# Lag table of a long convolution: half of its rows kept as two unsummed parts, lag products for two channels at once

## The chip, the cores and the metric

The kernel runs on one core of a Trainium2 chip. The metric is the device time of one execution in microseconds, the median over runs. A core has a matrix engine (TensorE; PE in the profile, with its weight loads as PEld), a vector engine (VectorE, DVE), an activation engine (ScalarE, ACT), GpSimd (POOL, hardly used here) and a queue of DMA issues (SyncE, SP).

## The reference

The output is `g * a + (1 - g) * b`. Here `a` is segmented causal attention with a compressive memory (2048 tokens in 4 segments of 512, 32 heads of 16 channels), `b` a long convolution of the same input with a kernel K per channel, and `g` a gate per token. Only the part that makes K is touched:

```python
dt = jnp.exp(log_dt)[:, None]
A = A_re + 1j * A_im
Bc = B_re + 1j * B_im
Cc = C_re + 1j * C_im
logdA = dt * A
dB = dt * Bc
l = (lambda x, dt: x.astype(dt))(jnp.arange(L), A_re.dtype)
P = jnp.exp(logdA[:, :, None] * l[None, None, :])
K = jnp.einsum('dn,dnl,dn->dl', Cc, P, dB).real
...
Yf = Uf * Kf[None, :, :, :]
```

There are 512 channels d, 128 states n and 2048 lags l. The lags are bf16 numbers, so that only 640 different ones occur. The kernel computes K at these alone, and the convolution as a transform over blocks.

## The kernel before

**Order by hand.** The program is a list of operations (PE, ACT, DVE, DMA). A search made ahead of time chose the sequence in which all of them are issued, and for operations that ACT or DVE can do (evacuations of PSUM and copies) which of the two does them; it stands in the string `ORDER`, one number for each operation, with `a` or `v` for the engine and the buffer slots behind slashes. `Sched.replay` (L235) puts each operation in its engine's program in this sequence, and `Sched.emit` adds the semaphores. The cost expressions beside the operations (`("V2", 256 * n)`, `c_pe("C", ...)`) are for that search and change nothing in the program. Every matmul is recorded at L686, every DMA at L222, evacuations at L226 (ACT) and L227 (DVE), evacuations with a scale at L229 and L230.

**Attention.** For each of 4 segments and 4 groups of heads: projections of q and k; five score products (`scores`, L1007) with 16 or 32 rows in four row strips of the array, all into one PSUM buffer of four banks; an exp over all of it (L1068, ACT, 80 of them); a mask product (L1080, DVE); products with v (17 columns each); normalisation (L1040 to L1043).

**K's tables.** `ssm_prep` transposes the six parameter arrays so that states are on partitions and channels in columns, and evacuates them (three evacuations of 1024 columns); `ssm_powers` squares exp(logdA) step by step; `ssm_cb` multiplies C by dB. `tables(c)` runs for c = 0 to 3, a quarter of the channels (128) each. A lag is written as the sum of one of 20 exponents (`F_EXP`) and one of 32 (`G_EXP`). F holds the powers for the 20, G those for the 32, times C dB; each element is complex (two planes) and has 128 channels, thus 256 values on each partition. `cmul` makes n new elements out of n known ones, a complex product in three DVE instructions of 256 n elements: the source times the real part of the power into the table (L1165), the source times the imaginary part into `t2` (L1168), and the sum of both with the planes of `t2` exchanged (L1172). There are 13 such calls a table: three with n = 1, four with n = 2, three with n = 4 and three with n = 8.

**Lag products.** For every channel, two products over the 128 states (real and imaginary plane) give 32 x 20 lags: G's 32 columns of that channel are the weights, F's 20 columns move. Four channels, 32 apart, stand in four column groups of the array. That is 256 matmuls a table, issued in 8 groups of 32. Two evacuations of 320 columns bring them to `kex` (two buffers), four DMAs to `KTT`, from which the convolution's K products read. F and G have one buffer each, so the next table begins when the lag products of this one are done.

**Convolution and end.** 32 units of K product (5 x 512 columns), elementwise product Y (L1281), inverse product V (2 x 512 columns), with their evacuations; then the final products with `wo` and the transform's last step. All K products need all four tables.

Of the kernel before, what the change touches and what calls it, by code (L numbers as in the profile page):

```python
# [7 lines left out]
ACT = mybir.ActivationFunctionType  # L8
# [360 lines left out]
0/0 10/0 9/1 23/0/0 24v 15/0 29/0 31/0 38/1 32/2 30/3 33/4 13/2 14/3 27/4/1 39/5 37/6 34 35 40/7 54/0 57/1 6/0 36  # L369
193/0 4/0 41 42 43 44/8 48/0 45/9 46/10 12/4 47 49/11 53/0 50/12 17/0 61/1 59/0 62v/0 51/13 58a/0 60 71/1 52 65/2 11/5  # L370
55/2 56v 73/2 7/0 74v/1 25/3/2 26a 200/5/0/0 201a 250/0/1/1 72 83/3 1247/1 1250/6/0 214/1/0/0 28v 215 75 86v/2 205/0
85/3 173/4 3/0 21/0 66/5 16/0 253/2/0 84 95/0 178/6 20/0 18/0 97/7 98a/3 1226/0 176/1 1/0 251a 96 107/2 63 181/3
1248/7 254a 109/0 1249a 22/0 99 110v/4 202 67 189/0 108 377/0 208/3 190 177/0 252 203/0/1 204a 174/0 196/2 255/0/1/1
191 1251a 119/2 240/0/0 87 79/1 241 120/2 111 209a 122v/5 100 121 123 394/3/1 179/1 256 175 257 133/3 182 88 242
996v/0 395a 131/2 124 132 219/0/1 220 221 146a/6 77/0 998v/0 134v/7 192/0 1003/0 135 143/3 206/3 76 995v 212/0 1002
228/0/2 217 64 994v 1004 145/7 997v 213a 112 1008 1009/1 144 216 1252 229 230 78 1010 210/0 211a 1000/0 223/0/3 224
197/0 198/0 1015/1 147 158v/8 1014 999 136 1016 157/4 207a 235/1 1229/2/1 159 89/2 1001 1012/1 225 222/0 1017 155/3
1230a 1237/3/0 1018/0 1238a 799/0 266/0/1 267 293/2/2/2 226 156 1005 227 231 199/0 268 1011 91/0 1013 236/0/3 167a/9
148 1026 294a 237 588/0 589/3 590 160 168 1020 238 1021/1 232/0 169 90 233 334/2/0/0 335a 1019 1227/3 1228a 234/0
262/0/2 263 1231 264 337/2/2 338a 1022 800/3 239 243 244 1239/0 1240a 245/1 1241 101/0 1029 271/0/3 272 1024/0 273 801  # L380
378/2 246 379 1023 296/0/1 1234/3/1 247 1232/2 1233a 283/0/0 1025 284 297a 391 258 1235a 285 218/1/0 1033/1 102/6 103
113/3 295 1032 259 1258/2/0 1006/0 1259a 1034 1236 260/0 265/0 115/2 1030/1 1244/3/1 279/0/2 280 281 1245a 1242/1
1243a 269 1260/2 1007 1261a 270 1262 274 275/2 1031 1036/0 1027/1 307/0/1 308 309 278/3 282 286 287 1035 288/3
298/1/0/0 299 276 248/2 1037 249a/0 114 125/2 320/0/3 321 322 1028 1038/2/0 300 301 289 127/3 290/1 180 1039 1040 336
1246 126 1041 1042v 139/7 339/1/1/1 340 341 1263/3/0 194 1264a 303/0/2 304 1043/2 1044 277 137/0 1253/3/1 1265/1 138
342 1045 1046 305 151/4 291/0 1254a 1052v/0 1055v 324/0/0 68v/0 325 1056v/0 1053v 302/3 1054v 1060 343 1061/0 292a
1057 1047a 1051/0 326 104v/3 1062 383/0/1/1 384a 306/2 105 346/0/2 1066 1058/1 347 1067/0 1059 344 1268/0 80v/1 1070/1
1255/3 106 1068 1266a 1267 1063 81 310 311 348 1073/0 400/0/0/0 1069 401 116v/4 1072 443/1/0 1071 1256a 1257 444a
312/0/1 1074 313 314 386/3/1 402 1078 490/1/2/2 491a 92a/5 349/0 387a 1079/1 1076/0 350/0/2 351 352 1080 1075 1082/1
# [72 lines left out]
def fft_consts():  # L462
# [35 lines left out]
    return W1, M2, N2, G2  # L498


F_EXP = [1, 3, 5, 7, 2, 4, 6, 8, 258, 260, 262, 264, 516, 520, 772, 776, 1032, 1288, 1544, 1800]
G_EXP = [8 * j for j in range(32)]


# [20 lines left out]
def build_graph(nc, es, A_x, A_wq, A_wk, A_wv, A_wo, A_beta, B_A_re, B_A_im, B_B_re, B_B_im,  # L525
# [95 lines left out]
    zsP = mkpool("zs", 2048, 2)  # L621
    H1 = a
    Z1T = Tile(S.pool('Z1', H1, 2048, 1, 0), F32)
    a += 13 * 1024
    H2 = a
    V2aP = mkpool("V2a", 16384, 1)
    T0 = a
# [802 lines left out]
```

## Time and profile before

| | us |
|---|---|
| median of three runs (304.58 to 305.8) | 305.31 |
| the profiled execution | 305.48 |
| its span, first to last instruction | 303.3 |
| PE busy | 263.6 (87%) |
| DVE busy | 264.7 (87%) |
| ACT busy | 263.1 (87%) |
| mean granted PE clock | 0.958 |
| first K product of the convolution starts at | 172.64 |

The table products (L1165, L1168, L1172) take 33.9 + 33.7 + 33.8 us of DVE. The lag products are 1024 matmuls of 128 rows, 32 weight columns and 20 moving columns, with 10.4 us of busy time in which several of them overlap. A matmul record's duration is its whole way through the array; how fast products follow one another is read from their starts. Three engines are equally full over the whole span, which says nothing of the single stages: shares of the span are means over stages with different limits.

### The profile page before, as it was taken

What the parts mean: (1) busy time and instruction counts of PE and PEld (TensorE: products, weight loads), DVE (VectorE), ACT (ScalarE), POOL (GpSimd) and SP (SyncE); (2) the same over time, 40 slices, a digit from 0 to 9 for tenths busy, and PEclk for the clock granted to TensorE, in tenths of its full rate; (3) what the DMA queues carried; (4) which work ended last, traced back from release to release, by engine and by line L of the source; (5) the groups of instructions that cost most, each with busy time, mean ns of one, the idle gap of its engine ahead of it and who ended that gap; (6) DMA issues with size and microseconds to landing.
All of it is one profiled execution on the core that took longest, in us unless ns stands there. A gap on an engine that the chain in (4) does not pass through costs nothing.

```text
span 303.3 us, 9592 instructions
## 1 busy us (share of the span) xinstructions
PE 263.6 (87%) x4078; PEld 150.3 (50%) x4078; DVE 264.7 (87%) x639; ACT 263.1 (87%) x315; POOL 3.2 (1%) x9
## 2 busy tenths in 40 slices
PE   2697698799687888788889999999999999999992
PEld 1442355665344544565446555555545455546551
DVE  2999999999999998999998799999999869957171
ACT  3999999999999899999989998998899999985321
POOL 2000000000000000000000000000000000000000
PEclk9999899789996879999979999999999999999999
DMA  6983722216012331630500516766767756741033
GB/s 150 276 216 90 130 73 71 71 28 185 19 52 53 111 98 40 197 93 17 134 2 18 145 59 197 208 197 180 210 169 212 200 157 187 208 143 46 11 152 126
DMA packets 45002, 37.37 MB, mean 123 GB/s; under 512 B 21408, under 2 KB 40864, under 8 KB 44960
## 3 DMA queue, kind: packets, MB, share of 16 engines
q1 hardware_dynamic: 44960, 36.77, 43.0%
q8 instruction: 32, 0.52, 0.7%
q14 instruction: 10, 0.08, 0.1%
HBM read 18.54 MB, written 6.29 MB: 82 GB/s over the span
## 4 chain that ended last, share of the span: by engine, by line
PE 52%; DVE 22%; ACT 17%; DMA 4%; issue 2%; SPq 1%; ACTq 0%
PE psum L686 51%; ACT sb L1068 9%; DVE sb L1168 5%; DVE sb L1172 5%; ACT sb L226 4%; DVE sb L1165 4%; DMA sb<-in_A_wo_dram 2%; DMA sb<-in_B_log_dt_dram 1%; ACT sb L794 1%; SPq L222 1%; DMA sb<-sb 1%; ACT sb L948 1%; ACT sb L802 1%; DVE sb L227 1%; DVE sb L1122 1%
## 5 line engine op out<-in xcount | busy, mean ns | idle before, releaser
L686 PE MATMUL psum<-sb 128*32 128x20 bf16 (+11 forms) x3990 | 256.4, 232 | 26.0 <-ACT sb L1068 15.0
L686 PEld LDWEIGHTS psum<-sb 128*128 128x128 bf16 (+3 forms) x3990 | 143.6, 97 | 136.6 <-ACT sb L1068 30.0
L1068 ACT ACTIVATE sb<-psum 128x2048 bf16<-128x2048 f32 x80 | 151.4, 1893 | 7.4 <-PE psum L686 6.4
L226 ACT ACTIVATE sb<-psum 128x512 bf16<-128x512 f32 (+2 forms) x152 | 86.1, 615 | 6.8 <-PE psum L686 6.2
L227 DVE CAST sb<-psum 128x512 bf16<-128x512 f32 (+1 forms) x50 | 32.9, 674 | 6.1 <-PE psum L686 5.6
L1165 DVE TENSOR_TENSOR sb<-sb 128x512 bf16<-128x512 bf16 (+3 forms) x52 | 33.9, 660 | 0.1
L1172 DVE TENSOR_TENSOR sb<-sb 128x512 bf16<-128x512 bf16 (+3 forms) x52 | 33.8, 662 | 0.2
L1168 DVE TENSOR_TENSOR sb<-sb 128x512 bf16<-128x512 bf16 (+3 forms) x52 | 33.7, 658 | 0.1
L1080 DVE TENSOR_TENSOR sb<-sb 128x1024 bf16<-128x1024 bf16 (+1 forms) x40 | 22.5, 575 | 1.1 <-ACT sb L1068 0.8
L1281 DVE TENSOR_TENSOR sb<-sb 128x1024 bf16<-128x1024 bf16 x32 | 21.8, 685 | 1.2 <-ACT sb L226 0.8
L229 ACT ACTIVATE sb<-psum,sb 128x512 bf16<-128x512 f32 (+1 forms) x8 | 5.4, 688 | 13.4 <-PE psum L686 13.4
L1043 DVE TENSOR_TENSOR sb<-psum,sb 128x256 bf16<-128x256 f32 x32 | 13.2, 419 | 0.4
L230 DVE TENSOR_SCALAR sb<-psum,sb 128x512 f32<-128x512 f32 (+1 forms) x8 | 6.0, 748 | 8.4 <-PE psum L686 8.3
L794 ACT ACTIVATE sb<-sb 128x512 f32<-128x512 f32 x18 | 11.7, 667 | 0.0
L1040 DVE RECIPROCAL sb<-psum 128x16 f32<-128x16 f32 x32 | 8.0, 250 | 1.7 <-PE psum L686 1.7
L742 PE MATMUL psum<-sb 128*128 128x128 bf16 x24 | 3.1, 309 | 6.8 <-DMA sb<-in_B_A_re_dram 4.1
L1122 DVE TENSOR_TENSOR sb<-psum,sb 128x512 bf16<-128x512 f32 x12 | 8.3, 688 | 0.3
L1338 DVE SCALAR_TENSOR_TENSOR sb<-psum,sb 128x512 bf16<-128x512 f32 x8 | 5.5, 746 | 3.0 <-PE psum L686 3.0
L948 ACT ACTIVATE sb<-psum 128x512 bf16<-128x512 bf16 x12 | 7.7, 638 | 0.5 <-PE psum L945 0.4
L795 DVE TENSOR_TENSOR sb<-sb 128x256 f32<-128x256 f32 x18 | 7.4, 416 | 0.5 <-ACT sb L794 0.5
L999 ACT ACTIVATE sb<-sb 128x512 bf16<-128x512 bf16 x12 | 7.6, 633 | 0.0
L796 DVE SCALAR_TENSOR_TENSOR sb<-sb 128x256 f32<-128x256 f32 x18 | 7.5, 417 | 0.0
(67 smaller groups left out, 105.1 us busy)
## 6 DMA issues: line engine op xcount, KB each, us to landing
sb<-sb SPq DMA_DIRECT2D x64, 128.0 KB, 3.1
sb<-c_DN SPq DMA_DIRECT2D x32, 224.0 KB, 3.1
scr_Z<-sb SPq DMA_DIRECT2D x16, 256.0 KB, 2.4
sb<-scr_Z SPq DMA_DIRECT2D x16, 256.0 KB, 3.5
sb<-in_A_x_dram SPq DMA_DIRECT2D x5, 512.0 KB, 4.6
out_dram<-sb SPq DMA_DIRECT2D x8, 256.0 KB, 2.0
sb<-sb SPq DMA_DIRECT2D x20, 64.0 KB, 2.2
sb<-c_M SPq DMA_DIRECT2D x4, 256.0 KB, 4.4
```

The source lines that it names most:

```text
L226: fa = lambda e: e.activation(dst(), src(), ACT.Copy)
L227: fd = lambda e: e.tensor_copy(dst(), src())
L686: mm = lambda e, o_, l, r_, st, sp, **kw: e.matmul(o_, lhsT=l, rhs=r_, start=st, stop=sp, skip_group_check=True, **kw)
L794: op("ACT", ("As", 512), lambda e, sq=sq, Z=Z: e.activation(ap(sq, n=512), ap(Z, n=512), ACT.Square), r=[Z], w=[sq], key=PW[h] + PWS * k)
L1043: op("DVE", ("V1", 256), lambda e: e.tensor_tensor(ap(o1, gi * 16, [[128, 4], [32, 4], [1, 16]]), ap(T, dims=[[68, 4], [17, 4], [1, 16]]), ...
L1068: o = op("ACT", ("Ax", 2048), lambda e, P=P, pT=pT: e.activation(ap(pT, n=2048), ap(P, n=2048), ACT.Exp, scale=0.25), r=[P], w=[pT])
L1080: op("DVE", ("V2", 128 * nb), lambda e, pT=pT, dims=dims: e.tensor_tensor(ap(pT, dims=dims + [[1, 128]]), ap(pT, dims=dims + [[1, 128]]), ...
L1122: op("DVE", ("V1", 512), lambda e: e.tensor_tensor(ap(o2, 0, [[128, 4], [16, 8], [1, 16]]), ap(P2, 0, [[256, 4], [17, 8], [1, 16]]), ap(R2 ...
L1165: op("DVE", ("V2", 256 * n), lambda e: e.tensor_tensor(run(tile, ne, dst, 1), run(tile, ne, src, sstep), ap(pw, cl * 512, [[2, 128], [0, n ...
L1168: op("DVE", ("V2", 256 * n), lambda e: e.tensor_tensor(run(t2, n, 0, 1), run(tile, ne, src, sstep), ap(pw, cl * 512 + 256, [[2, 128], [0, ...
L1172: op("DVE", ("V2", 256 * n), lambda e: e.tensor_tensor(D_(), D_(), ap(t2, n * 128, [[-n * 128, 2], [2 * n, 64], [1, 2 * n]]), ALU.add), r= ...
L1281: op("DVE", ("V2", 1024), lambda e, Y=Y, XAB=XAB, K3=K3, xo=xo: e.tensor_tensor(ap(Y, dims=[[512, 2], [1, 512]]), ap(XAB, xo, [[512, 2], [ ...
```

## The change

- `F_EXP` has the same 20 exponents in another sequence, so that two calls of `cmul` with n = 1 become one with n = 2. A table has 12 calls.
- G's rows change halves: the smaller 16 exponents are now rows 16 to 31, the larger ones (128 and up) rows 0 to 15. For rows 0 to 15 (two calls with n = 8) the third instruction of `cmul` is left out: the first part stays in G, the second in a new buffer `GB` in place of `t2`, and the lag products add them up in PSUM.
- The lag products take two neighbouring channels at once. Weights are G's 64 columns of both (two planes) and then GB's 32 columns of both (two planes); 40 columns of F move. Each product gives all pairs of the two channels, of which those of a channel with itself are used. Two pairs of channels stand side by side, in column positions 0 and 64. There are 256 matmuls a table as before, in groups of 32, and three evacuations (480, 480 and 320 columns). The four DMAs read every second partition.
- The transposed parameters and `dt` are written in a sequence of channels in which channels 32 apart become neighbours; the diagonal's products follow (16 of one column for 4).
- `kex` has one buffer of double size; the pools of squares, Z, V2a and Xs lie elsewhere, with three squares instead of four and six Z instead of eight.
- `ORDER` is another one throughout, with 1730 operations instead of 1746.

The diff, without the lines of `ORDER`:

```diff
--- before.py
+++ after.py
@@ -366,92 +366,91 @@
 ORDER = """
...
 """
@@ -498,8 +497,8 @@
     return W1, M2, N2, G2
 
 
-F_EXP = [1, 3, 5, 7, 2, 4, 6, 8, 258, 260, 262, 264, 516, 520, 772, 776, 1032, 1288, 1544, 1800]
-G_EXP = [8 * j for j in range(32)]
+F_EXP = [1, 3, 6, 8, 2, 4, 262, 264, 258, 260, 5, 7, 520, 516, 776, 772, 1032, 1288, 1544, 1800]
+G_EXP = [128 + 8 * j for j in range(16)] + [8 * j for j in range(16)]
 
 
 def dft_const():
@@ -621,15 +620,15 @@
     zsP = mkpool("zs", 2048, 2)
     H1 = a
     Z1T = Tile(S.pool('Z1', H1, 2048, 1, 0), F32)
-    a += 13 * 1024
-    H2 = a
-    V2aP = mkpool("V2a", 16384, 1)
+    a += 2048
+    GBP = mkpool("GB", 8192, 1)
+    a = H1 + 29 * 1024
     T0 = a
     FP = mkpool("F", 10240, 1)
     GP = mkpool("G", 16384, 1)
     t2P = mkpool("t2", 4096, 2)
     pwP = mkpool("pw", 2048, NPW)
-    kexP = mkpool("kex", 1280, 2)
+    kexP = mkpool("kex", 2560, 1)
     TEND = a
     S.room = 207 * 1024 - a
     assert a <= 207 * 1024, a - 207 * 1024
@@ -638,9 +637,9 @@
     ftP = mkpool("ft", 1024, 14, 0)
     pbP = mkpool("pb", 2048, 3, 0)
     dtP = mkpool("dt", 1024, 1, 0)
-    a = H2 - 8192
-    sqPs = [mkpool("sq", 2048, 4, 0)] * 2
-    ZPs = [mkpool("Z", 2048, 8, 0)] * 2
+    a = H1 + 10 * 1024
+    sqPs = [mkpool("sq", 2048, 3, 0)] * 2
+    ZPs = [mkpool("Z", 2048, 6, 0)] * 2
     a = PT0
     prP = mkpool("pr", 1024, 6, 0)
     ldP = mkpool("ldt", 1024, 1, 0)
@@ -650,8 +649,9 @@
     MP = mkpool("M", 2048, 3, 2)
     assert a <= H1, a - H1
     a = H1
+    V2aP = mkpool("V2a", 16384, 1, 2)
     XsPs = [mkpool("Xsa", 4096, 3, 2)]
-    assert a <= H2, a - H2
+    assert a <= T0, a - T0
     a = T0
     V2bP = mkpool("V2b", 16384, 1, 2)
     CDP = mkpool("CD", 1792, 4, 2)
@@ -744,10 +744,10 @@
             T = Tile(pbP, BF16)
             S.tag = "prm%d" % wj
             op("PE", c_pe("F", *[128] * 8), f, r=[praw[2 * wj], praw[2 * wj + 1], ident], w=[P], acq=[T])
-            S.evac(lambda T=T: ap(T, n=1024), lambda P=P: ap(P, n=1024), 1024, r=[P], w=[T], psum16=True)
+            S.evac(lambda T=T: ap(T, 0, [[64, 16], [2, 32], [1, 2]]), lambda P=P: ap(P, 0, [[64, 16], [1, 32], [32, 2]]), 1024, r=[P], w=[T], psum16=True)
             pb.append(T)
         dt = Tile(dtP, BF16)
-        op("ACT", ("Asx", 512), lambda e: e.activation(ap(dt, n=512), ap(ldt, n=512), ACT.Exp), r=[ldt], w=[dt])
+        op("ACT", ("Asx", 512), lambda e: e.activation(ap(dt, 0, [[64, 8], [2, 32], [1, 2]]), ap(ldt, 0, [[64, 8], [1, 32], [32, 2]]), ACT.Exp), r=[ldt], w=[dt])
         res = []
         ers = []
         st = []
@@ -831,7 +831,8 @@
 
         def f(e):
             for c in range(4):
-                i = mm(e, ap(P, c, n=1), ap(CBT, 512 + c * 128, n=128), ap(onesT, n=1), True, True)
+                for q in range(4):
+                    i = mm(e, ap(P, c, n=1, p0=32 * q, np_=32), ap(CBT, 512 + c * 128 + 64 * (q // 2) + q % 2, [[2, 32]]), ap(onesT, n=1), True, True, tile_position=(0, 32 * q))
             return i
         op("PE", c_pe("F", 1, 1, 1, 1), f, r=[onesT] + CBp, w=[P])
         op("DVE", ("V1", 4), lambda e: e.tensor_tensor(ap(dcolT, n=4), ap(P, n=4), ap(dskT, n=4), ALU.add), r=[P, dskT], w=[dcolT])
@@ -1152,6 +1153,9 @@
                 res.append(dct[e_])
             return res
 
+        GB = Tile(GBP, BF16)
+        gbp = [GB.part() for _ in range(2)]
+
         def cmul(tile, dct, ne, dst, src, sstep, n, k):
             pw = pws[(k, h)]
             S.key = k0 + TT * 0.8 * nstep[0] / 50
@@ -1160,62 +1164,71 @@
             nstep[1] += 1
             rd = parts(dct, tile, src, n, sstep)
             wr = parts(dct, tile, dst, n)
-            t2 = Tile(t2P, BF16)
+            top = tile is G and dst < 16
+            t2 = GB if top else Tile(t2P, BF16)
+            tn, t0 = (16, dst) if top else (n, 0)
             run = lambda T, E, e0, st: ap(T, 2 * e0, [[2 * E, 128], [2 * st, n], [1, 2]])
-            op("DVE", ("V2", 256 * n), lambda e: e.tensor_tensor(run(tile, ne, dst, 1), run(tile, ne, src, sstep),
+            v2 = "V2n1" if n == 1 else "V2"
+            op("DVE", (v2, 256 * n), lambda e: e.tensor_tensor(run(tile, ne, dst, 1), run(tile, ne, src, sstep),
                                                                  ap(pw, cl * 512, [[2, 128], [0, n], [1, 2]]), ALU.mult),
                r=rd + [pw], w=wr + [tile])
-            op("DVE", ("V2", 256 * n), lambda e: e.tensor_tensor(run(t2, n, 0, 1), run(tile, ne, src, sstep),
+            op("DVE", (v2, 256 * n), lambda e: e.tensor_tensor(run(t2, tn, t0, 1), run(tile, ne, src, sstep),
                                                                  ap(pw, cl * 512 + 256, [[2, 128], [0, n], [1, 2]]), ALU.mult),
-               r=rd + [pw], w=[t2])
+               r=rd + [pw], w=[gbp[dst // 8]] if top else [t2])
+            if top:
+                return
             D_ = lambda: ap(tile, 2 * dst, [[ne * 128, 2], [2 * ne, 64], [1, 2 * n]])
-            op("DVE", ("V2", 256 * n), lambda e: e.tensor_tensor(
+            op("DVE", (v2, 256 * n), lambda e: e.tensor_tensor(
                 D_(), D_(), ap(t2, n * 128, [[-n * 128, 2], [2 * n, 64], [1, 2 * n]]), ALU.add), r=[t2], w=wr)
         fm = lambda *a_: cmul(F, fp, NF, *a_)
         gm = lambda *a_: cmul(G, gp, NG, *a_)
         k0 = S.key
         nstep = [0, 0]
         S.tag = "tabc%d" % c
-        for e_, k_ in ((0, 0), (4, 1), (5, 2), (7, 3)):
+        for e_, k_ in ((0, 0), (4, 1), (5, 2), (3, 3)):
             S.evac(lambda e_=e_: ap(F, 2 * e_, [[FPL, 2], [2 * NF, 64], [1, 2]]),
                    lambda k_=k_: ap(pws[(k_, h)], cl * 512, [[256, 2], [2, 64], [1, 2]]), 256,
                    r=[pws[(k_, h)]], w=parts(fp, F, e_, 1), pw=[F], sb=True)
-        S.evac(lambda: ap(G, dims=[[GPL, 2], [2 * NG, 64], [1, 2]]), lambda: ap(CBT, d0, [[512, 2], [2, 64], [1, 2]]), 256,
-               r=[CBp[h]], w=parts(gp, G, 0, 1), pw=[G], sb=True)
-        fm(1, 0, 1, 1, 1)
-        gm(1, 0, 1, 1, 3)
-        fm(2, 0, 1, 2, 2)
-        gm(2, 0, 1, 2, 4)
-        fm(6, 4, 1, 1, 2)
-        gm(4, 0, 1, 4, 5)
-        gm(8, 0, 1, 8, 6)
-        fm(8, 4, 1, 4, 8)
-        fm(12, 5, 2, 4, 9)
-        gm(16, 0, 1, 8, 7)
-        gm(24, 8, 1, 8, 7)
-        fm(16, 13, 2, 2, 9)
+        S.evac(lambda: ap(G, 32, dims=[[GPL, 2], [2 * NG, 64], [1, 2]]), lambda: ap(CBT, d0, [[512, 2], [2, 64], [1, 2]]), 256,
+               r=[CBp[h]], w=parts(gp, G, 16, 1), pw=[G], sb=True)
+        fm(1, 0, 5, 2, 1)
+        gm(17, 16, 1, 1, 3)
+        fm(10, 0, 1, 2, 2)
+        gm(18, 16, 1, 2, 4)
+        gm(20, 16, 1, 4, 5)
+        gm(24, 16, 1, 8, 6)
+        fm(6, 2, 1, 4, 8)
+        fm(12, 3, 2, 4, 9)
+        gm(0, 16, 1, 8, 7)
+        gm(8, 24, 1, 8, 7)
+        fm(16, 12, 2, 2, 9)
         fm(18, 16, 1, 2, 9)
         fr = [fp[i] for i in range(NF)]
-        gr = [gp[i] for i in range(NG)]
+        gr = [gp[i] for i in range(NG)] + gbp
         kex = Tile(kexP, BF16)
         S.key = k0 + TT * 0.8
         S.tag = "lag%d" % c
-        for hf in range(2):
+        for b0, nb in ((0, 12), (12, 12), (24, 8)):
             P = S.ps()
-            for sl0 in range(0, 16, 4):
-                def f(e, P=P, hf=hf, sl0=sl0):
+            for sl0 in range(0, nb, 4):
+                def f(e, P=P, b0=b0, sl0=sl0):
                     for sl in range(sl0, sl0 + 4):
-                        for cc in range(2):
-                            for dq in range(4):
-                                dl = 32 * dq + 16 * hf + sl
-                                i = mm(e, ap(P, sl * NF, n=NF, p0=32 * dq, np_=32), ap(G, (1 - cc) * GPL + (dl // 2) * 2 * NG + dl % 2, [[2, NG]]),
-                                       ap(F, cc * FPL + (dl // 2) * 2 * NF + dl % 2, [[2, NF]]), cc == 0, cc == 1, tile_position=(0, 32 * dq))
+                        for q in range(2):
+                            for cc in range(2):
+                                for hh in range(2):
+                                    pr = 32 * hh + b0 + sl
+                                    if q == 0:
+                                        w, m = ap(G, (1 - cc) * GPL + pr * 2 * NG, n=2 * NG), 64
+                                    else:
+                                        w, m = ap(GB, cc * 2048 + pr * 32, n=32), 32
+                                    i = mm(e, ap(P, sl * 40, n=40, p0=64 * hh, np_=m), w,
+                                           ap(F, cc * FPL + pr * 2 * NF, [[1, 2], [2, NF]]), q == 0 and cc == 0, q == 1 and cc == 1, tile_position=(0, 64 * hh))
                     return i
-                op("PE", c_pe("C", *[20] * 8), f, r=fr + gr + [F, G], pw=[P], acq=[kex])
-            S.evac(lambda hf=hf: ap(kex, 16 * hf, [[32, NF], [1, 16]]), lambda P=P: ap(P, dims=[[1, NF], [NF, 16]]), 320, r=[P], pw=[kex])
+                op("PE", c_pe("C", *[40] * 32), f, r=fr + gr, pw=[P], acq=[kex])
+            S.evac(lambda b0=b0, nb=nb: ap(kex, b0, [[32, 40], [1, nb]]), lambda P=P, nb=nb: ap(P, dims=[[1, 40], [40, nb]]), 40 * nb, r=[P], pw=[kex])
         for dq in range(4):
             S.dma(lambda dq=dq: ap(KTT, (4 * c + dq) * 160, n=160),
-                  lambda dq=dq: ap(kex, n=640, p0=32 * dq, np_=32), 40960, r=[kex], pw=[KTp[c // 2]])
+                  lambda dq=dq: ap(kex, 640 * (dq % 2), n=640, p0=64 * (dq // 2) + dq % 2, np_=32, pstep=2), 40960, r=[kex], pw=[KTp[c // 2]])
 
     def conv(k0, dk):
         D = dft_const().reshape(128, 16, 2, 5, 128).transpose(2, 1, 0, 3, 4).reshape(32, 128, 640)
```

## The prediction

> **What bounds the kernel now.** I read the windows view first, cut where the chain of waits changes character: 13.57 us is the first projection, 172.64 us the first K product of the convolution. Columns: stretch, its length, then busy time (and instructions) of PE, PEld, DVE, ACT and POOL, the granted clock, the DMA share and GB/s.
>
> ```profile
> 13.57:165.99 152.42, 127.61 (x2568) 75.58 (x2569) 148.16 (x379) 146.45 (x183) 1.31 (x2) 0.92 0.32 86
> 165.99:172.64 6.65, 6.26 (x88) 3.65 (x82) 5.29 (x14) 6.29 (x7) 0.00 (x0) 1.00 0.45 110
> 172.64:298.05 125.41, 124.75 (x1388) 67.14 (x1388) 103.12 (x228) 102.44 (x114) 0.00 (x0) 1.00 0.55 162
> ```
>
> There are two kernels in one. In the first 152 us VectorE (DVE) is busy 97% and ScalarE (ACT) 96%, and TensorE (PE) has 25 us free. After the first K product PE is busy 124.75 of 125.41 us, and nothing else matters. Second, the groups of the first stretch:
>
> ```profile
> L686 PE MATMUL psum<-sb 128*32 128x20 bf16 (+10 forms) x2528 | 125.6, 218 | 25.0 <-ACT sb L1068 15.0 <-DVE sb L1043 3.0 <-DVE sb L1172 1.9
> L1068 ACT ACTIVATE sb<-psum 128x2048 bf16<-128x2048 f32 x45 | 85.6, 1903 | 2.4 <-PE psum L686 1.8
> ```
>
> Of PE's 25.0 us, 15.0 end at an exponential (L1068): all scores share one PSUM buffer of four banks, so PE cannot write the next scores before the exp has read these, and ACT's exp needs PE at once after. Third, the chain of waits where the stretches meet (start, length, what):
>
> ```profile
> 161.77 5.77 PE psum L686 x223
> ...
> 167.62 0.59 SPq L222
> ...
> 168.90 0.60 SPq L222
> ...
> 169.54 3.01 DMA sb<-sb
> 172.55 0.09 issue
> 172.64 1.65 PE psum L686 x21
> ```
>
> The last lag products, their evacuation, four DMA issues, a landing, then K. So the time is (when the last table's lag products are done) + 6.65 us + (PE's work from the first K on). Last, the prices, from the groups by form:
>
> ```profile
> L1172 DVE TENSOR_TENSOR sb<-sb 128x2048 bf16<-128x2048 bf16 x12 | 14.5, 1212 | 0.0
> ...
> L1172 DVE TENSOR_TENSOR sb<-sb 128x512 bf16<-128x512 bf16 x16 | 6.7, 419 | 0.0
> ...
> L1168 DVE TENSOR_TENSOR sb<-sb 128x512 bf16<-128x512 bf16 x16 | 6.6, 412 | 0.0
> L1165 DVE TENSOR_TENSOR sb<-sb 128x512 bf16<-128x512 bf16 x16 | 6.5, 415 | 0.0
> ...
> L1172 DVE TENSOR_TENSOR sb<-sb 128x256 bf16<-128x256 bf16 x12 | 5.0, 412 | 0.1
> L1165 DVE TENSOR_TENSOR sb<-sb 128x256 bf16<-128x256 bf16 x12 | 4.9, 410 | 0.0
> L1168 DVE TENSOR_TENSOR sb<-sb 128x256 bf16<-128x256 bf16 x12 | 4.8, 396 | 0.0
> ...
> L226 ACT ACTIVATE sb<-psum 128x320 bf16<-128x320 f32 x6 | 2.7, 447 | 0.1
> ```
>
> A product over one exponent (256 elements) costs what one over two does (512).
>
> **The change, part by part.** (1) *Sums left out.* The adds of two G calls of eight exponents go, in four tables: 8 x 1.212 = 9.7 us of DVE. (2) *F's sequence.* Two one-exponent calls become one of two: 8 x (410+396+412) - 4 x (415+412+419) ns = 4.8 us. DVE is freed of 14.5 us. (3) *Evacuations.* Instead of two of 320 elements a table there are two of 480 and one of 320. Between 447 ns (320) and 617 ns (512) a 480 costs about 590: 590+590+447-2x447 = 0.73 us a table, 2.9 us in all, nearly all on ACT. (4) *The new order* hands DVE some of ACT's evacuations: ACT has 162 instead of 172, DVE 103 instead of 89. Pricing every operation that stands before the first K by its row: ACT 180.2 -> 176.6 us (one exp less), DVE 195.9 -> 190.3. These are sums of means, which overlap; ACT's busy time is 0.91 of its sum, DVE's 0.85. So both engines have 3.3 and 4.8 us less to do before the first K; I take 4.0 us earlier, if PE keeps up. (5) *From the first K on* PE's work at its pace in the records (216 ns for 512 columns, 56 for 128, 25 for 17) is 122.1 us before and 121.2 after: -0.9. (6) *Small things.* The three parameter evacuations (683 ns on DVE, about 1 us on ACT) now read with a step of 32: between nothing and twice as long, +0.7 each, partly under the waits for input loads: 0. The diagonal has 16 products of one column for 4: 0.3 us, off the path. One kex buffer for two: the next table's evacuation comes over 15 us after these four DMAs, whose landing takes 2 to 3 us: 0; if the last of them were still queued, one landing, 3 us. The DMAs keep count and size and their last place before the first K. V2a and Xs lie elsewhere; what lies under them is done before their first evacuation: 0.
>
> (7) *The lag products* are the open price. There are 256 a table as before, but of another kind. Before: 32 weight columns, 20 moving columns, four side by side in four column groups. In the records four start every 27 ns at full clock (122 of them in 956 ns from 164.67 us): 32 of them, one group of the order, take 0.22 us. After: two side by side, and for every pair of channels four products with 64 weight columns and then four with 32. A group of 32 is thus eight batches of four. Low end: each pair of products costs a round of 27 ns, 16 x 27 = 0.43 us. High end: PE changes from a 64-column to a 32-column division at every batch, and a change costs what changes cost in this trace. Where lag products with nothing to wait for are followed by a full 128-column matmul, the next start comes 104 to 115 ns after the last one instead of 7 (97.396 to 97.511 us, 165.809 to 165.920); score products in four row strips followed by transposes: 317 ns instead of 216. So a batch takes 27 + 110 ns and a group 1.10 us, five times today's. No row shows a change from 64 to 32; every change of division in the trace is charged, so I take the high end. The 32 groups then add 32 x 0.88 = 28 us to PE in a stretch where it has 25 free.
>
> The Trainium skill, TensorEngine Tiling (Array Packing), section Key Properties, says that changing the tiling mode, not only the tile, drains TensorE; the rows of 104 to 115 ns agree, and by the rule the sum is the one below, without it that of rival A. The skill's page TensorE: Matmul & The Clock Gate, section on LDWEIGHTS, lets a weight load grow with its columns (P/1.2 ns), which fits the 27 ns round; 64 columns would then need 53 ns, an estimate of 0.65 us a group even where no change is charged, and 1.3 where it is.
>
> What a group of 1.10 us delays: behind the bursts stand scores, thus an exp. In the new order the groups come in bursts of 3, 5, 5, 3, 3, 3, 2, 5, 3. While PE is in one, ACT has one exp in hand (1.9 us) and about half of its other work per exp ((146.45 - 85.6)/45 = 1.35 us): 2.6 us. Bursts of five (5.5 us) leave ACT without work for 2.9 us, of three (3.3 us) for 0.7: 3 x 2.9 + 5 x 0.7 = 12.2 us. DVE cannot run ahead either, since the next table needs the F and G buffers that the lag products still read.
>
> **Sum**, on the profiled execution's span: 303.3 - 4.0 - 0.9 + 12.2 = 310.6 us; 2.2 us lie around the span (305.48 us) and the median of the runs is 0.2 lower: **312.6 us**.
>
> **Rivals.** *A, the changes of division are free* (64 and 32 columns are one mode, or the sequencer hides it). A burst of five takes 2.2 us, less than ACT has in hand; only the gains are left: 305.3 - 4.0 - 0.9 = 300.4 (299.6 by DVE's gain, 301.1 by ACT's). For it: lag products today overlap in four column groups without loss, and DVE is the fullest engine of the stretch. Against it: no change in the trace is free. It decides the sign: below some 0.7 us a group the bursts of five cost no more than 3 us and the kernel is faster. 30%. *B, the price is real, but hidden*: PE's 25 free us and the evacuations in hand cover the bursts but for some 4 us; 305.3 - 4.9 + 4.9 = 305.3. Against it: 15 of the 25 us are waits for the exp which a late score brings back. 11%. *C, PE becomes the bound of the first stretch*: 127.6 + 28 = 155.8 us of work, and the 15 us of waits at the exps stay: +18.4 - 0.9 = 322.8; a fuller PE would lose less at half clock (0.92 granted now), so some 320. For it: 155.8 is already over 152.4. 15%. The forecast: 44%.
>
> **Range and chances.** 299.5 to 321 us: the low end is A with DVE's gain, the high end C; 8 in 10 or a little more. The forecast's own range, from in-hand work of 1.9 us instead of 2.6 (18.1 us lost) to 3.5 (6 us lost), is 306.4 to 318.5. About 0.5% (1.5 us) is what a measurement of this kernel can tell from no change. Faster: A, 0.30; same: B, 0.11; slower: the forecast and C, 0.59.
>
> **What would show it.** The lag rows: 1024 products of 40 columns whose busy time is about 30 to 38 us (mine) or 14 (A) where 10.4 was; starts in batches of four with 110 ns between batches. In the first stretch ACT's idle before L1068 grows from 2 to over 12 us, released by PE, and the first K comes near 181 us (A: 169). The table products' busy time falls by 14.5 us whatever happens. PE's stretch from the first K on stays at 124 to 125 us. I am wrong if lag products of both widths follow each other at the even pace of 27 ns a round, or if ACT stays full beside slow ones.

## The result, and the profile after

| | before | after |
|---|---|---|
| median, us (4 runs each) | 304.94 (304.21 to 305.8) | 345.49 (343.68 to 347.29) |
| ratio, 95% interval | | 1.1328 (1.1257 to 1.14) |
| span of the profiled execution, us | 303.3 | 345.5 |
| mean granted PE clock | 0.958 | 0.897 |
| first K product of the convolution, us | 172.64 | 214.36 |

The direction was as forecast; the size was not: 40 us where 7 were forecast, outside the range. The windows view, cut at the first projection and at the first K product (columns as before: stretch, length, busy time and instructions of PE, PEld, DVE, ACT and POOL, granted clock, DMA share, GB/s), says at once where:

```profile
13.57:172.64 159.07, 133.87 (x2650) 79.23 (x2651) 153.46 (x392) 152.74 (x189) 1.31 (x2) 0.92 0.32 87
```

That is the first stretch before the change. After it:

```profile
13.57:214.36 200.79, 172.72 (x2658) 111.24 (x2684) 152.88 (x388) 152.60 (x185) 1.31 (x2) 0.83 0.27 74
214.36:340.00 125.64, 123.01 (x1347) 65.86 (x1364) 103.96 (x227) 100.73 (x109) 0.00 (x0) 1.00 0.54 153
```

From the first K product on nothing has changed (125.6 us for 125.4). All of the loss, 41.7 us, is ahead of it, and there VectorE and ScalarE are as busy as they were (152.9 and 152.6 us; before 153.5 and 152.7). It is PE that has 38.9 us more (172.7 for 133.9). In slices of 20 us the loss has places of its own. The first row is from the kernel before, the others from the changed one:

```profile
60.00:80.00 20.00, 18.16 (x374) 10.92 (x362) 19.61 (x51) 19.97 (x26) 0.00 (x0) 0.93 0.30 87
```

```profile
60.00:80.00 20.00, 18.52 (x321) 13.45 (x323) 9.48 (x30) 11.01 (x14) 0.00 (x0) 0.58 0.08 23
80.00:100.00 20.00, 14.91 (x213) 8.40 (x214) 19.91 (x40) 20.00 (x25) 0.00 (x0) 1.00 0.24 76
100.00:120.00 20.00, 19.62 (x342) 13.53 (x341) 9.86 (x38) 9.67 (x12) 0.65 (x1) 0.68 0.21 57
140.00:160.00 20.00, 18.39 (x316) 14.11 (x320) 10.73 (x35) 10.74 (x15) 0.00 (x0) 0.74 0.19 56
```

Between the lag products (80 to 100 us) DVE and ACT are full as before. In the slices that hold them both stand still half of the time, PE is busy, and its granted clock is 0.58 to 0.74. The groups, by form (line, engine, operation, operands, count, busy us, mean ns, idle before and what ended it). The first row is the exps of the kernel before:

```profile
L1068 ACT ACTIVATE sb<-psum 128x2048 bf16<-128x2048 f32 x80 | 151.4, 1893 | 7.4 <-PE psum L686 6.4
```

```profile
L686 PE MATMUL psum<-sb 128*64 128x40 bf16 x512 | 34.5, 214 | 3.0 <-DVE sb L1181 2.1 <-DVE sb L804 0.9
L686 PE MATMUL psum<-sb 128*32 128x40 bf16 x512 | 30.3, 197 | 0.0
...
L1069 ACT ACTIVATE sb<-psum 128x2048 bf16<-128x2048 f32 x80 | 151.0, 1887 | 17.0 <-PE psum L686 16.1
...
L226 ACT ACTIVATE sb<-psum 128x480 bf16<-128x480 f32 x7 | 4.0, 570 | 22.4 <-PE psum L686 22.4
```

The lag rows are busy for 34.5 and 30.3 us, where 30 to 38 for both together was forecast. ACT's idle time before the exps (L1069) has grown from 7.4 to 17.0 us (ahead of the first K product from 2.4 to 14.2), and 22.4 us more stand before the evacuations of the lag products themselves. The timeline around the second burst, of five groups, shows what one does (start, length, engine, line, operation; in brackets the idle time before it and who ended it):

```profile
61.45 1.13 ACT L226 ACTIVATE sb<-psum 128x480 bf16<-128x480 f32 x2 [2.73 <-PE psum L686]
61.88 10.46 PE L686 MATMUL psum<-sb 16*128 16x384 bf16 x184 [0.47 <-issue]
...
63.50 1.88 ACT L1069 ACTIVATE sb<-psum 128x2048 bf16<-128x2048 f32 x1 [0.40 <-PE psum L686]
...
68.81 0.57 ACT L226 ACTIVATE sb<-psum 128x480 bf16<-128x480 f32 x1 [3.44 <-PE psum L686]
72.07 0.44 ACT L226 ACTIVATE sb<-psum 128x320 bf16<-128x320 f32 x1 [2.69 <-PE psum L686]
72.07 0.30 DVE L227 COPY sb<-sb 128x256 bf16<-128x256 bf16 x1 [7.12 <-PE psum L686]
```

PE works for 10.46 us without a pause: a few scores and transposes, and then 8.0 us of lag products, named in the row by the first of the 184 only. ACT has one exp in that time (to 65.38 us) and then waits 3.44 and 2.69 us, each time for a bank of lag products; DVE waits 7.12 us with a copy that begins the next table and needs the buffers that the lag products still read. At 72.07 us both start again.

The starts of the products in the trace, in the burst near 100 us while it still has the full clock, show the price of one pair of channels. From the first of four products with 64 columns to the first with 32 it is 171 ns, from there to the next 64 it is 151, then 172 and 153. Two batches take 322 ns, a group of 32 products (four pairs) 1.29 us; at half clock a pair takes 406 ns, a group 1.62 us. From first to last start all nine bursts take 45.7 us; before the change the lag products took 8.0 (pauses over 0.3 us left out).

On the other side of the account the table's DVE groups are these:

```profile
L1172 DVE TENSOR_TENSOR sb<-sb 128x512 bf16<-128x512 bf16 x20 | 9.0, 451 | 0.0
L1175 DVE TENSOR_TENSOR sb<-sb 128x512 bf16<-128x512 bf16 x20 | 9.0, 448 | 0.0
L1172 DVE TENSOR_TENSOR sb<-sb 128x1024 bf16<-128x1024 bf16 x12 | 8.8, 737 | 1.1 <-DMA sb<-sb 1.1
...
L1181 DVE TENSOR_TENSOR sb<-sb 128x2048 bf16<-128x2048 bf16 x4 | 4.9, 1217 | 0.0
```

Four sums of 2048 elements are left of twelve, as the change says. But the multiplications of 512 and 1024 elements have become dearer (415 and 686 ns before); see the run of F's sequence alone. The rows of three experiments below are those of disturbed executions at a lower granted clock: "two changes" (315.25 us, the other three 310.6 to 311.1), "four changes" (325.92 us; of the others one took 322.95, two 317.8 and 318.1) and "the sums put back" (318.25 us, the fastest 309.28).

### The profile page after: what moved, and what is told of

The parts are those of the page before. It is cut to its first block, busy times and chain, and to the rows that moved or that the text cites. A ratio compares the mean times of both kernels' runs of the same rounds, so it can differ in the third digit from the quotient of the medians.

```text
span 345.5 us, 9550 instructions
## 1 busy us (share of the span) xinstructions
PE 301.0 (87%) x4042; PEld 181.4 (53%) x4090; DVE 264.8 (77%) x633; ACT 260.6 (75%) x305; POOL 3.2 (1%) x9
## 4 chain that ended last, share of the span: by engine, by line
PE 58%; DVE 26%; ACT 8%; DMA 4%; issue 2%; SPq 0%; DVEq 0%
PE psum L686 57%; DVE sb L1175 6%; DVE sb L1172 6%; ACT sb L1069 6%; DVE sb L1181 4%; ACT sb L226 2%; DVE sb L227 2%; DMA sb<-c_DN 1%; DMA sb<-in_B_log_dt_dram 1%; DVE sb L795 1%; DMA sb<-sb 1%; PE psum L946 1%; DVE sb L796 1%; DVE sb L804 1%; DVE sb L950 0%
## 5 line engine op out<-in xcount | busy, mean ns | idle before, releaser
L686 PE MATMUL psum<-sb 128*128 128x17 bf16 (+10 forms) x3954 | 293.3, 240 | 30.1 <-ACT sb L1069 13.7
L686 PEld LDWEIGHTS psum<-sb 128*128 128x128 bf16 (+4 forms) x4002 | 174.4, 103 | 147.6 <-ACT sb L1069 29.0
L1069 ACT ACTIVATE sb<-psum 128x2048 bf16<-128x2048 f32 x80 | 151.0, 1887 | 17.0 <-PE psum L686 16.1
L226 ACT ACTIVATE sb<-psum 128x512 bf16<-128x512 f32 (+2 forms) x145 | 82.9, 611 | 39.5 <-PE psum L686 39.0
L227 DVE CAST sb<-psum 128x512 bf16<-128x512 f32 (+1 forms) x61 | 41.0, 684 | 28.8 <-PE psum L686 24.4
L1172 DVE TENSOR_TENSOR sb<-sb 128x512 bf16<-128x512 bf16 (+3 forms) x48 | 33.6, 710 | 1.2 <-DMA sb<-sb 1.1
L1175 DVE TENSOR_TENSOR sb<-sb 128x512 bf16<-128x512 bf16 (+3 forms) x48 | 33.1, 707 | 0.1
L1081 DVE TENSOR_TENSOR sb<-sb 128x1024 bf16<-128x1024 bf16 (+1 forms) x40 | 22.6, 574 | 0.8 <-ACT sb L1069 0.6
L1181 DVE TENSOR_TENSOR sb<-sb 128x512 bf16<-128x512 bf16 (+3 forms) x40 | 22.6, 575 | 0.1
L229 ACT ACTIVATE sb<-psum,sb 128x512 f32<-128x512 f32 (+1 forms) x8 | 5.4, 688 | 14.0 <-PE psum L686 14.0
L227 DVE COPY sb<-sb 128x256 bf16<-128x256 bf16 x18 | 5.1, 317 | 12.0 <-PE psum L686 12.0
```

The source lines that it names most:

```text
L226: fa = lambda e: e.activation(dst(), src(), ACT.Copy)
L227: fd = lambda e: e.tensor_copy(dst(), src())
L686: mm = lambda e, o_, l, r_, st, sp, **kw: e.matmul(o_, lhsT=l, rhs=r_, start=st, stop=sp, skip_group_check=True, **kw)
L1069: o = op("ACT", ("Ax", 2048), lambda e, P=P, pT=pT: e.activation(ap(pT, n=2048), ap(P, n=2048), ACT.Exp, scale=0.25), r=[P], w=[pT])
L1081: op("DVE", ("V2", 128 * nb), lambda e, pT=pT, dims=dims: e.tensor_tensor(ap(pT, dims=dims + [[1, 128]]), ap(pT, dims=dims + [[1, 128]]), ...
L1172: op("DVE", (v2, 256 * n), lambda e: e.tensor_tensor(run(tile, ne, dst, 1), run(tile, ne, src, sstep), ap(pw, cl * 512, [[2, 128], [0, n], ...
```

## The experiments

Theory at the start: the change of width inside the lag products (64 columns, 32 columns, eight times a group) sets their pace, and the time follows the number of changes. Rivals: wider products cost more as such; the new order and buffers are at fault. The edits are to the changed kernel unless another is named. Those expectations that were written before the first results go by this price alone.

**Two changes a group.** All 64-column products of a group first, then its 32-column ones:

```diff
-                    for sl in range(sl0, sl0 + 4):
-                        for q in range(2):
+                    for q in range(2):
+                        for sl in range(sl0, sl0 + 4):
```

> Theory: the excess is the change between 64 and 32 weight columns. In the changed kernel's records a batch of 64-wide products starts 171 ns, of 32-wide ones 151 ns before the next batch, where rounds inside a batch take 53 and 40 ns; so a group of 32 costs 1.29 us at full clock. With all 64-wide products of a group first and then all 32-wide ones there are two changes a group instead of eight: 7 x 53 + 118 + 7 x 40 + 111 = 0.88 us, 13 us less over the 32 groups, or 16 at the half clock of these stretches: 330 to 333 us. Rival 1 (the wider products themselves, the changes free): the same products stand here, 343 to 347 us. Rival 2 (the new order and the moved buffers): also unchanged, 343 to 347.

Measured: 311.0 us (310.58 to 315.25), ratio 1.0155 (1.0099 to 1.0212). With nothing changed but the sequence of products, 34 of the 40 us are gone, far more than the theory had expected: what goes is not the price of the changes alone. One part is the pace between changes, 31.8 and 25 ns a round instead of the 53 and 40 behind a change: a group takes 0.67 us at full clock where 0.88 was expected. The rest is PE's other work up to the first K product, 118.6 us for 127.0 in the profiled executions, with 30.4 us at half clock for 72.9.

**Four changes a group.** The same by two pairs of channels:

```diff
-                    for sl in range(sl0, sl0 + 4):
-                        for q in range(2):
+                    for q, sl in [(q, s + t) for s in (sl0, sl0 + 2) for q in range(2) for t in range(2)]:
+                        if True:
```

> Two pairs' 64-wide products, then their 32-wide ones: four changes a group, between the kernels with two (311.0 us) and eight (345.5). Theory (each change costs some 75 to 110 ns of a drained array, and the first stretch has nothing to cover it): a group lasts about 0.85 us where those two have 0.63 and 1.29 at full clock, 7 us more of products than with two changes: 317 to 323 us. Rival (the clock: the drained array is granted half its clock, and only the eight changes drain it enough): like two changes, 310 to 314 us, at 28 to 35 us of half clock instead of the changed kernel's 73; or, if the clock falls here too, 328 or more.

Measured: 320.55 us (317.8 to 325.92), ratio 1.0454 (1.0395 to 1.0513). As expected, by then from the two runs with two and no changes.

**One change a bank.** All 64-column products of a PSUM bank, then all its 32-column ones:

```diff
-                    for sl in range(sl0, sl0 + 4):
-                        for q in range(2):
+                    for q, sl in [(q, s) for q in range(2) for s in range(nb)][2 * sl0:2 * sl0 + 8]:
+                        if True:
```

> All 64-wide products of a PSUM bank (12 or 8 pairs), then all its 32-wide ones: about one change a group or less, the same sums as in the changed kernel. Theory: close to the kernel without any change (307.4 us): 306.5 to 309.5 us, some 0.53 us a group. Rival (alternation inside a group costs nothing by itself, and the kernel with two changes differs from the one with none by its narrower products): no better than 311.

Measured: 307.53 us (306.1 to 308.32), ratio 1.0106 (1.007 to 1.0141). It computes the same as the changed kernel and is 38 us faster, though not faster than the kernel before.

**No change inside a group.** The second part's products take 64 weight columns too, which adds wrong rows to the table:

```diff
-                                        w, m = ap(GB, cc * 2048 + pr * 32, n=32), 32
+                                        w, m = ap(GB, cc * 2048 + min(pr, 62) * 32, n=64), 64
```

> The second part's products take 64 weight columns too, so that the lower half of each table's rows gets a neighbouring pair's values added and the convolution is another one. No change of division is left inside a group. Theory: 16 rounds of 53 ns = 0.85 us a group, near the kernel with two changes: 329 to 332 us; starts evenly 53 ns apart in twos, no 110 ns gap. Rival 1 (wide products): more columns are loaded than in the changed kernel, so slower than it, 348 us or more. Rival 2 (order, buffers): 343 to 347.

Measured: 307.44 us (305.17 to 311.38), ratio 1.0054 (1.0018 to 1.009). More columns and no change: wider products as such are ruled out, and as with two changes the gain is far above the expected one. In the records two 64-column products side by side start every 31.8 ns.

**The second part left out.** Only the first part's products, 128 a table; the terms of `GB` are missing from the table:

```diff
-                        for q in range(2):
+                        for q in range(1):
...
-                                           ap(F, cc * FPL + pr * 2 * NF, [[1, 2], [2, NF]]), q == 0 and cc == 0, q == 1 and cc == 1, tile_position=(0, 64 * hh))
+                                           ap(F, cc * FPL + pr * 2 * NF, [[1, 2], [2, NF]]), q == 0 and cc == 0, cc == 1, tile_position=(0, 64 * hh))
```

> The second part's products are left out, so the upper half of the table's rows is not the sum. Products: 128 a table, eight rounds of 32 ns a group, 0.26 us, near the kernel before (0.26 us measured, with its waits). Theory (the lag products alone stand between the changed kernel and the gain worked out for DVE and the order): 300 to 303 us. Rival (the order or the slower table products and parameter evacuations cost the gain): 304.5 us or more, with the first K product no earlier than 171.5 us.

Measured: 301.3 us (299.81 to 302.61), ratio 0.9901 (0.9872 to 0.9929). Where the lag products take little more than before (9.7 us for 8.0), the kernel with its new order, buffers and DMAs is 3.7 us faster.

The dose, in one table (lag: from first to last start, summed over the bursts, pauses over 0.3 us left out; PE busy and free from 13.57 us to the first K product; the last five columns are of the profiled execution, which took 315.25 us with two changes and 325.92 with four):

| kernel | changes a group | time, us | lag, us | first K, us | PE busy | PE free | clock |
|---|---|---|---|---|---|---|---|
| before | | 304.94 | 8.0 | 172.64 | 133.9 | 25.2 | 0.92 |
| second part left out | 0 | 301.3 | 9.7 | 170.31 | 131.4 | 25.4 | 0.92 |
| no change | 0 | 307.44 | 17.5 | 173.56 | 133.2 | 26.8 | 0.97 |
| one change a bank | under 1 | 307.53 | 16.1 | 174.68 | 135.1 | 26.1 | 0.97 |
| two changes | 2 | 311.0 | 22.9 | 183.34 | 141.4 | 28.4 | 0.92 |
| four changes | 4 | 320.55 | 29.5 | 192.65 | 154.3 | 24.8 | 0.90 |
| after | 8 | 345.49 | 45.7 | 214.36 | 172.7 | 28.1 | 0.83 |

The rows of the windows view behind five of these lines, in this order: second part left out, no change, one change a bank, two changes, four changes.

```profile
13.57:170.31 156.74, 131.35 (x2170) 80.80 (x2169) 151.02 (x388) 149.76 (x183) 1.31 (x2) 0.92 0.35 92
```

```profile
13.57:173.56 159.99, 133.22 (x2657) 86.64 (x2684) 151.50 (x388) 150.35 (x184) 1.31 (x2) 0.97 0.33 89
```

```profile
13.57:174.68 161.11, 135.05 (x2682) 84.68 (x2681) 151.49 (x388) 150.75 (x183) 1.31 (x2) 0.97 0.33 88
```

```profile
13.57:183.34 169.77, 141.42 (x2655) 91.42 (x2682) 151.88 (x388) 151.05 (x184) 1.32 (x2) 0.92 0.31 83
```

```profile
13.57:192.65 179.08, 154.27 (x2684) 95.52 (x2683) 151.49 (x388) 151.07 (x182) 1.32 (x2) 0.90 0.30 82
```

The column to read is "PE free". Lag products of 9.7 to 45.7 us leave it at 25 to 28 us: no increase of PE's work has gone into PE's idle time. And from "no change" to "after", with one order and one division of labour, 28.2 us more of lag products move the first K by 40.8 us. PE's free time is 1.3 of it; the remaining 11.3 us are PE's other work, which goes from 133.2 - 17.5 = 115.7 to 172.7 - 45.7 = 127.0 us, while time at half clock goes from 14.9 to 72.9 us in the records. The first step of the dose looks different: from "second part left out" to "no change" 7.8 us more of lag products move the first K by only 3.3 us. That is not idle time put to use either, since PE's free time is 1.4 us longer; PE's other work is 6.0 us shorter there, with 14.9 us at half clock for 29.0. No run shows why the clock falls less.

**Only 32 columns.** A 64-column product as two of 32 side by side, 384 products a table, all of one width:

```diff
...
+                                    for lo in range(2 - q):
+                                        w = ap(GB, cc * 2048 + pr * 32, n=32) if q else ap(G, (1 - cc) * GPL + pr * 2 * NG + 32 * lo, n=32)
...
```

> The 64 columns of the first part are taken as two products of 32 in two column groups; 384 products a table, all 32 wide, the same sums. Theory: four rounds a pair of channels at 27 to 40 ns, 0.43 to 0.64 us a group instead of 1.29, 14 to 20 us in all instead of the 45.7 us that the nine bursts last: the first K product comes 25 to 32 us earlier, 313 to 321 us; if what is left of the bursts is hidden again behind the exps, down to 302. Rival 1 (wide products: 40 moving columns and more of them): no better than 335. Rival 2 (order, buffers): 343 to 347.

Measured: 316.62 us (315.86 to 317.67), ratio 1.0346 (1.0292 to 1.04). Within the expected range; but the products run at some 8.4 ns each and take 13.1 us (pauses over 0.3 us left out), less than the 16.1 in "one change a bank", and still the first K comes at 182.89 us. The next run shows why.

**One channel at a time**, as before the change, with G's 32 columns and then `GB`'s 16, 512 products a table:

```diff
-                                        w, m = ap(G, (1 - cc) * GPL + pr * 2 * NG, n=2 * NG), 64
+                                        w, m = ap(G, (1 - cc) * GPL + pr * 2 * NG + b, [[2, NG]]), 32
...
-                                        w, m = ap(GB, cc * 2048 + pr * 32, n=32), 32
+                                        w, m = ap(GB, cc * 2048 + pr * 32 + b, [[2, 16]]), 16
...
```

> The two parts stay unsummed, but each channel is taken alone again: 32 and then 16 weight columns, 20 moving ones, four column groups, 512 products a table, evacuations of 240, 240 and 160 columns. No change of division. Theory: 128 rounds of 27 ns, 3.5 us a table, 14 us in all, and less evacuation: 0 to 5 us faster than the kernel with 32-wide pairs; 300 to 315 us. Rival 1 (wide products) predicts the same gain here, since none is left: this run does not tell it from the theory. Rival 2 (order, buffers): 343 to 347.

Measured: 329.85 us (329.33 to 330.81), ratio 1.0779 (1.0726 to 1.0833), outside what was expected. PE's waits (engine and what, released by; us in total, times, longest) show a thing that no other kernel has so much of:

```profile
PE psum L686 <- issue: 23.3, 22, 2.4
PE psum L686 <- ACT sb L1069: 13.4, 20, 2.0
```

For 23.3 us PE waits for nothing that the profile shows. The rows of the products, by form, say where:

```profile
L686 PE MATMUL psum<-sb 128*32 128x20 bf16 x1024 | 18.9, 180 | 17.3 <-issue 15.1 <-DVE sb L1181 1.2 <-DVE sb L804 0.9
L686 PE MATMUL psum<-sb 128*16 128x20 bf16 x1024 | 18.3, 174 | 3.3 <-issue 3.3
```

So 18.4 of the 23.3 us lie among the lag products; the first three stalls last 2.0, 2.2 and 2.2 us. Counting weight loads and matmuls, there are 255 and 256 PE instructions from one of them to the next (further on 251 to 256, 509 to 511, 1,019, 1,269 and 1,527 between stalls over 0.3 us among lag products: about 1, 2, 4, 5 and 6 times 256). "Only 32 columns" has 11.5 us of the same kind, the changed kernel 2.7. So this is not what the change lost its time to. It is of the size by which these two ways around the changes of width fall behind "one change a bank" (22.3 us for 23.3 of stalls, 9.1 for 11.5).

**F's sequence alone**, in the kernel before, with its order but for the 12 instructions that go:

```diff
-        fm(1, 0, 1, 1, 1)
+        fm(1, 0, 5, 2, 1)
...
-        fm(6, 4, 1, 1, 2)
...
-        fm(12, 5, 2, 4, 9)
+        fm(12, 3, 2, 4, 9)
```

> The kernel before with F's new sequence alone: two one-exponent calls become one of two, 12 calls a table, everything else and its order as before. Theory (DVE, the fullest engine of the first stretch, sets its end): 4.8 us less of DVE, 1 to 4 us of it in the time: 301 to 304 us. Rival (ACT is as full, 96%, and its work is the same): 304.5 to 306 us.

Measured: 304.74 us (303.22 to 306.46), ratio 0.9995 (0.9962 to 1.0028): nothing. The groups of this run show one reason:

```profile
L1188 DVE TENSOR_TENSOR sb<-sb 128x512 bf16<-128x512 bf16 x20 | 9.0, 453 | 0.0
L1191 DVE TENSOR_TENSOR sb<-sb 128x1024 bf16<-128x1024 bf16 x12 | 8.9, 744 | 0.0
...
L1188 DVE TENSOR_TENSOR sb<-sb 128x1024 bf16<-128x1024 bf16 x12 | 8.9, 742 | 0.0
```

Two calls are dearer in the new sequence. The call that reads F's columns 0 and 5, `fm(1, 0, 5, 2, 1)`, takes 586 to 616 ns a multiplication in all four tables, where other calls of 512 elements take some 415; the one that reads columns 3, 5, 7 and 9 takes 840 to 858 instead of the 685 of columns 5, 7, 9 and 11 before. By line, the three instructions of `cmul` are 33.8 + 33.6 + 32.5 = 99.9 us, for 101.4 before: 1.5 us freed instead of 4.8. In the changed kernel the same two groups stand at 451 and 737 ns. The rival, that ACT is as full as DVE and holds the time, is not settled by this run.

**The sums put back.** The changed kernel's order with the eight sums put in, and the whole table from the first part's products alone:

```diff
             if top:
+                D_ = lambda: ap(tile, 2 * dst, [[ne * 128, 2], [2 * ne, 64], [1, 2 * n]])
+                op("DVE", (v2, 256 * n), lambda e: e.tensor_tensor(
+                    D_(), D_(), ap(GB, 2048 + 2 * dst, [[-2048, 2], [32, 64], [1, 2 * n]]), ALU.add), r=[gbp[dst // 8]], w=wr)
                 return
...
-                        for q in range(2):
+                        for q in range(1):
...
```

> The changed kernel with its sums put back: VectorE adds the second part to rows 0 to 15 of G as before the change (8 instructions of 2048 elements more, just behind the two products), and the lag products take G's 64 columns of a channel pair only (128 products a table, no change of width). It computes the whole table; the sequence of F, the new order and the 14 evacuations given to VectorE stay. Theory: the gain that the run with the second part's products left out showed (301.3 us) is VectorE's time, and the new order has spent it on those evacuations; with 8 x 1.22 = 9.8 us of sums back the first K moves from 170.1 to 176 to 180 us and the time is 306.5 to 311 us. Rival: the gain is the new order's, and the sums were hidden: 300 to 303 us.

Measured: 309.28 to 318.25 us in six runs, five of them 317 to 318; too uneven for an interval. The lowest is 8.0 us above the median with the sums left out (301.3), so the rival (the order alone brings the gain) falls. The size rests on this one run, which is in the theory's range; the median of all six, 317.26 us, is above it. The first stretch of the profiled run (318.25 us):

```profile
13.57:186.38 172.81, 138.60 (x2169) 85.32 (x2168) 161.18 (x396) 150.61 (x183) 1.32 (x2) 0.87 0.31 82
```

DVE has 161.2 us of work here instead of 151.0, and PE is free for 34.2 us.

## Why the prediction was wrong

**The lag products' price** was right in its mechanism and too low: 1.29 us a group at full clock for 1.10. The gap from the last product of a batch to the next batch is 116 ns behind 64 columns and 110 behind 32, just as charged from neighbouring rows. What was too small is the round, two products side by side, in front of it: 27 ns were taken, from 32-column products with 20 moving columns, and the second round of a batch starts 52 and 39 ns after the first. (Even for the old products the prediction's own line, 122 starts in 956 ns, gives 31 ns for four and not 27.) Without changes a round takes 31.8 ns with 64 columns and 25 with 32, in the long runs of "one change a bank", so four products of each take 64 + 50 = 114 ns; with two changes they take 322, and a change costs 104 ns. Besides, half of the products ran at half clock. Instead of 28 us PE got 37.6 more.

**The cover is the step that failed**: "While PE is in one, ACT has one exp in hand (1.9 us) and about half of its other work per exp ...: 2.6 us", and with it "3 x 2.9 + 5 x 0.7 = 12.2 us". It hid 15.8 of the 28 us. The runs show no such cover: against 25.2 us before the change, PE's free time is between 24.8 and 28.4 us in every line of the table, and more where PE stalls. In the timeline above ACT did have its one exp, but the burst of five lasted 8.0 us instead of 5.5, and ACT waited 6.1 us in it instead of 2.9; DVE, to whose waits the forecast gave no number, stood for 7.1. The sum up to the first K was 28.0 - 15.8 - 4.0 = 8.2 us; it became 37.6 (lag) + 1.2 (PE's other work, 125.8 to 127.0 us) + 2.9 (PE free) = 41.7 us. Of the 33.5 us between the two, 15.8 are the cover, 9.6 the size of the lag products, 4.0 the gain, of which nothing is left once PE sets the pace, and 4.1 the other two terms.

**Half clock** was no term of the forecast for these bursts. PE's records look busy in them, yet the granted clock falls to 0.58 in the slice 60 to 80 us. Against "no change" PE's other work is 11.3 us longer; against the kernel before, which has 27.7 us of half clock itself, only 1.2.

**The gain** was there, but smaller. The sums are gone as forecast (8 of 1.22 us, 9.8 us). F's sequence frees 1.5 us instead of 4.8. By line the table products fell from 101.4 to 33.6 + 33.1 + 22.6 = 89.3 us, 12.1 instead of 14.5. With cheap lag products the first K comes 2.3 us earlier, not 4.0, and the whole is 301.3 us, close to rival A's 300.4. The order turns the freed time into this gain only with the sums left out (309.28 us at the least with them back), and F's sequence without a new order brings nothing.

**From the first K on**: -0.9 was forecast, and it is +0.2 us in the profile after and -0.6 with the second part left out (124.85 us); a small term, right within 1.1 us. **Small things**: the parameter evacuations on DVE take 1042 ns for 683, 0.36 us more each where 0 to 0.7 was allowed, and no run shows that the end feels it.

**The rivals.** A (changes are free) falls by the 104 ns. B (hidden) falls with the cover. C had the right mechanism, PE as the bound with its waits for the exp left in place, at 15%. Its own sum with measured sizes, all 25 us of free time kept and 37.6 us of lag, is 305.3 + 37.6 = 342.9 us; with 1.2 us of other work, 2.9 of free time and 0.2 behind the first K it is 347.2, where the profiled execution took 347.29. It had been set at 322.8 with 28 us of lag products and 15 of the 25 us kept.

The Trainium skill, TensorEngine Tiling (Array Packing), section Key Properties, says that a change of tiling mode drains TensorE. The runs agree: going between 64 and 32 columns costs like such a change, 322 ns with it and 114 without. The estimate of 53 ns for a load of 64 columns, from the Trainium skill, TensorE: Matmul & The Clock Gate, section on LDWEIGHTS, fits the first round behind a change (52 ns, though 32 columns, 27 ns by the same formula, take 39 there), and the 1.3 us a group estimated from it with the changes charged came out at 1.29. It does not hold for the pace of a steady run: 31.8 ns a round here, with two loads in it.

**What stays open.** Why the calls with other column distances are dearer on DVE. How much of the lost cover belongs to F and G having one buffer each (DVE's 7.12 us wait) and how much to the length of the bursts: bursts split up, or a second pair of buffers, were not tried. No version here that computes the whole table beats the kernel before; the nearest is "one change a bank" at 307.53 us.

## What to carry to other kernels

When small matmuls of different widths share the array, put all of one width together before the next: the same 256 products a table took 45.7 us for four tables in one sequence and 16.1 in another, and the sequence cost nothing. An engine's idle time is cover only if the work that is added can run while the others keep going; idle time that is a wait for another engine's answer comes back behind every added microsecond, so charge the whole of it unless a queue of ready work is seen in the trace. And price a reordering of table columns by its access pattern, not only by its number of elements: here it ate 3 of 5 us.

## What the runs showed of the hardware

**A stall every 256 PE instructions.** Lag products at 8 ns each, a weight load and a matmul, run into stalls of up to 2.4 us that come 256 weight loads and matmuls apart, or a multiple of it (waits for nothing shown: 23.3 us in "one channel at a time", 11.5 in "only 32 columns", 2.7 in the changed kernel). Among the DMA records, a packet of 16,384 bytes on an instruction queue starts 0.2 to 0.3 us before each of the first three stalls, takes 0.9 to 1.0 us, and the stall ends 2.3 to 2.4 us after its start. The Trainium skill, Runtime: NRT & Kernel Launch, section Instruction fetch mechanics, describes refills in blocks of 16 KiB, 256 instructions, and calls them mostly hidden; the runs agree on the block and show that 256 instructions of some 4 ns, about 1 us of work, do not hide one.

**A busy PE at half clock.** In the slice 60 to 80 us PE is busy for 18.5 of 20 us and is granted 0.58 of its clock, while the slice 80 to 100 us, with 14.9 us of busy time, has 1.00. Busy time in the records is thus no sign of a full clock: in batches between changes the records overlap (214 and 197 ns each, eight in 322 ns), while the same eight take 114 ns in long runs of one width. Five of the nine bursts have the clock fall to half while they run; in "one change a bank" no lag product runs at half clock. What the clock answers to is not shown beyond that.
